# Two interleaved accumulation groups whose upper and lower rows share banks, and a gate of one VectorE product

## The chip, the cores and the metric

The kernel runs on one core of one Trainium2 chip. The metric is the time of one execution on the device in microseconds (us); less is better. The core has TensorE (PE in the profile; PEld is its weight load), VectorE (DVE), ScalarE (ACT), GpSimd (POOL), SyncE (SP), which only issues transfers, and 16 DMA engines. [...]

## What is computed

The reference has two stages over 8 batches of 3200 rows:

```
scores = (1/3200) * z @ z.T            # z: 8 x 3200 x 64
attn   = max(scores, 0) ** 2
x      = u * (attn @ v)                # u, v: 8 x 3200 x 256
wq, wk = x @ w_q, x @ w_k              # 256 -> 64
mixed  = (wq @ wk.T / 8) @ x
out    = max(mixed, 0) @ w_out
```

The kernel never forms `wq @ wk.T`: it sums `wk.T @ x` (64 x 256) over a batch, and multiplies `wq` by that sum later. Nearly all of the work is in the first stage.

## The kernel before, in words

**Tiles.** A batch is cut into 7 groups of output rows (`widths`, L39: six of 512 and one of 128) and 25 tiles of 128 rows (`NT`). For a group `gi` and a tile `ti`, `scores` (L218) multiplies z by itself into PSUM, two tiles at a time (460 such pairs in all), `first_stage` (L238) applies the relu on ScalarE (L242) or VectorE (L246) and leaves `g`, and `second_stage` (L252) squares `g` on ScalarE (L259) or GpSimd (L261) into `at`, an fp16 tile. `at` comes from a ring of `NAT` = 14 buffers (L52). Since the scores are symmetric, a part of the blocks is not computed twice: SyncE issues a transposing DMA from `at` into `tt` tiles (L281), and `weights` (L289) takes a row either from `at` or from `tt`.

**The second product** (`second_product`, L296) multiplies the 128 x 128 blocks of `at` by `v`. Every product is split by rows: the upper 64 partitions (r = 0) and the lower 64 (r = 1) run as two matmuls side by side on the two row halves of the array. [...] A half group (two of the four blocks, `half`) thus has two banks, `acc{half}0` and `acc{half}1`, and one group takes all four accumulation banks (`pacc`). The other four banks hold two `ps` tiles for everything else. A group takes its rows some eight at a time, first for one half, then for the other (`open_rows`, L759); one group is open at a time, and the next begins when the halves' banks are free.

**The gate** (`gate`, L312) runs once per half group: ScalarE copies `acc{half}0` to SBUF (L318), VectorE adds `acc{half}1` (L319), GpSimd multiplies by `u` and writes `x_sb` (L334). For the last two groups VectorE makes a second, dense product (L328). `x_sb` is then transposed by DMA (L348), projected (L365), its keys are transposed (L383) and doubled (L395), and the heads are summed (L402). A batch later come the mixing (L430), the output projection (L457), its eviction by ScalarE (L485) into one of two `fo` buffers, and the store (L486).

**The order** of all instructions is written by a planner in Python, which keeps a clock for each engine: `use_pair` (L584) emits scores, `squares` (L597) chooses ScalarE or GpSimd for each square, `acc_step` (L804) emits two matmuls of the second product, `half_done` (L737) emits the gate and plans the transpose of x, `calm` (L818) holds scores back just before a half group closes, and `move`/`send` (L544, L547) put the transfers into SyncE's queue by due times. The main loop (L866) chooses the next piece of TensorE's work. Every engine then executes its instructions in the order written.

Of the kernel before, what the change touches and what calls it, by code (L numbers as in the profile page):

```python
# [16 lines left out]
def kernel(  # L17
# [34 lines left out]
    NAT = 14  # L52
    NX = 6
    NEARBY = 8
# [10 lines left out]
    psum = ctx.enter_context(tc.tile_pool(name="psum", bufs=3))  # L65
# [11 lines left out]
    def acc_tile(half, r, name, dtype=FP32):  # L77
        n = W if dtype == FP32 else 2 * W
        return pacc.tile([P, n], dtype, tag=f"acc{half}{r}", name=name)

    def top(r):
        return slice(r * dqk, (r + 1) * dqk)
# [204 lines left out]
    accs, xds = {}, {}  # L287
# [8 lines left out]
    def second_product(b, gi, half, ti, first, last):  # L296
        js = range(2 * half, min(2 * half + 2, widths[gi] // P))

        def one(j, r):
            if first and j == js[0]:  # L300
                accs[half, r] = acc_tile(half, r, f"acc{half}{r}")
            nc.tensor.matmul(  # L302
                out=accs[half, r][:, ds((j % 2) * D, D)],
                lhsT=weights(b, gi, ti, j)[top(r), :],
                rhs=vs[b][top(r), ti, :],
                start=(first and j == js[0]),
                stop=(last and j == js[-1]),
            )

        return [lambda j=j: [one(j, r) for r in range(2)] for j in js]  # L310

    def gate(b, gi, half):  # L312
        if (b, gi) not in xs:
            assert len(xs) < NX, (b, gi, list(xs))
            xs[b, gi] = px.tile([P, 2, NC, 2, dh], FP16, tag="x_sb", name="x_sb")
        n = min(2, widths[gi] // P - 2 * half)
        both = psum.tile([P, 2 * D], FP32, tag="both", name="both")
        nc.scalar.copy(out=both[:, 0 : n * D], in_=accs[half, 0][:, 0 : n * D])  # L318
        nc.vector.tensor_add(  # L319
            out=both[:, 0 : n * D], in0=accs[half, 1][:, 0 : n * D], in1=both[:, 0 : n * D]  # L320
        )
        if b == B - 1 and gi >= LASTG - 1:
            if gi < LASTG and half == 0:
                spare = pz.tile([P, NT, 2, dqk], FP16, tag="zd", name="xd")
                spare = spare[:].rearrange("p n a k -> p (n a k)")
                xds[LASTG - 1] = spare[:, 0 : 4 * D].rearrange("p (n d) -> p n d", d=D)
                xds[LASTG] = spare[:, 4 * D : 5 * D].rearrange("p (n d) -> p n d", d=D)
            nc.vector.tensor_mul(  # L328
                out=xds[gi][:, 2 * half : 2 * half + n, :].rearrange("p n d -> p (n d)"),
                in0=both[:, 0 : n * D],  # L330
                in1=us[b, gi][:, 2 * half : 2 * half + n, :].rearrange("p n d -> p (n d)"),
            )
        for r in [half] if widths[gi] == W else range(2):
            nc.gpsimd.tensor_mul(  # L334
                out=xs[b, gi][:, 0:n, :, r, :].rearrange("p n c d -> p (n c) d"),
                in0=both[:, 0 : n * D].rearrange("p (m d) -> p m d", d=dh),
                in1=us[b, gi][:, 2 * half : 2 * half + n, :].rearrange(
                    "p n (c d) -> p (n c) d", d=dh
                ),
            )  # L340
        if 2 * half + n == widths[gi] // P:
            us.pop((b, gi))
# [15 lines left out]
    def halves(gi):  # L358
        return range((widths[gi] // P + 1) // 2)
# [372 lines left out]
    GUARD = 12  # L732
    XDUE = 5.0
    XWAIT = 3.0
    LATE = 0.3

    def half_done(b, gi, half):  # L737
        ready = clock[PE] + FROM_PE
        t = give(ACT, ready, 0.57)
        t = give(DVE, t, 0.68)  # L740
        free_at[half] = t
        t = give(POOL, t, 1.2)
        gate(b, gi, half)
        if half == halves(gi)[-1]:
            n = 8 if widths[gi] == W else 2
            move(
                t + SLACK, t + XDUE, 1.28, 0.21 * n, lambda: turn_x(b, gi),
                lambda t: x_landed(t, b, gi), lambda: len(xTs) < 3,
            )
# [6 lines left out]
    current = {}  # L756
    work, used = [], set()

    def open_rows():  # L759
        if not current.get("left"):  # L760
            if not groups:
                return False
            b, gi = groups.pop(0)
            current.update(b=b, gi=gi, left=list(range(NT)), fresh=True)
            group_begun(b, gi, clock[PE])
        b, gi, left, fresh = (current[x] for x in ("b", "gi", "left", "fresh"))
# [3 lines left out]
        mine = [t for t in ready if (b, gi, t) in made]  # L770
        closing = len(left) <= NEARBY + 1
        want = len(left) if closing else NEARBY
        take = (mine + [t for t in ready if t not in mine])[:want]
        if len(take) < want:
            if closing and len(left) - len(take) < 4:
                take = take[: len(left) - 4]
            if not take or (fresh and len(take) < (6 if b or gi else 2)):
                return False
            if not closing:
                take = take[: max(0, len(left) - 4)]  # L780
        for t in take:
            left.remove(t)
        order = list(halves(gi))
        if fresh and gi == 0 and b > 0:
            order.reverse()
        for half in order:
            for t in take:
                first, end = fresh and t == take[0], not left and t == take[-1]
                todo = second_product(b, gi, half, t, first, end)
                for i, fn in enumerate(todo):  # L790
                    final = i == len(todo) - 1
                    work.append(
                        (
                            fn,
                            (b, gi, half),
                            first and i == 0,
                            end and final,
                            (b, gi, t) if final and half == order[-1] else None,
                        )
                    )  # L800
        current["fresh"] = False
        return True

    def acc_step():  # L804
        if not work and not open_rows():
            return False
        fn, (b, gi, half), begins, closes, row = work[0]
        if begins and free_at.get(half, 0.0) > clock[PE]:
            return False
        work.pop(0)  # L810
        fn()
        clock[PE] += 0.1093 * cold()
        used.add(row)
        if closes:
            half_done(b, gi, half)
        return True

    def calm(weight):  # L818
        steps = next((i for i, x in enumerate(work[:GUARD]) if x[3]), None)
        if steps is None:  # L820
            return True
        shut = clock[PE] + 0.1093 * steps
        first = min(clock[ACT], clock[DVE])
        return max(first, clock[PE] + 0.5) + weight <= shut + LATE

# [7 lines left out]
    make_identity(nc, ident)  # L833
    load_first_z()
# [16 lines left out]
    current.update(b=0, gi=0, left=list(range(NT)), fresh=True)  # L851
    groups.pop(0)
# [7 lines left out]
    group_begun(0, 0, 12.0)  # L860

    total = B * sum(NT * (w // P) for w in widths)
    done_acc = 0
    lead = 140
    turn_about = False
    while groups or work or current["left"]:  # L866
# [18 lines left out]
        wanted = able and p * total < (done_acc + lead) * NPAIR  # L885
        room = room and calm(1.1)
        if room and extra and (not wanted or turn_about or extra[1] == "proj"):
            turn_about = False
            extras.remove(extra)
            extra[2]()  # L890
        elif room and wanted:
            turn_about = True
            use_pair()
        elif acc_step():
            done_acc += 1
# [109 lines left out]
```

## Time and profile before

| | |
|---|---|
| time, median of 3 runs | 803.41 us (803.13 to 806.71) |
| span of the profiled execution | 804.1 us, 0.7 us above that median |
| TensorE busy | 774.2 us, 96% of the span |
| GpSimd busy | 627.2 us, 78% |
| ScalarE busy | 579.3 us, 72% |
| VectorE busy | 467.7 us, 58% |

A busy time is the time in which at least one of an engine's instructions was under way. Since matmuls overlap, TensorE's busy share does not say how near it is to its best pace; the waits, which tell what the engine stood idle for, and the pace of a long run of equal matmuls say more. The chain of work goes back from the last instruction to what released each step. For transfers the profile gives the time of issue on a queue and the landing.

### The profile page before, as it was taken

The numbers are of one execution on the slowest core, as the hardware profiler recorded it, in microseconds if no ns is written. First come the engines' busy times: TensorE is split into PE (matmuls) and PEld (weight loads), VectorE is DVE, ScalarE is ACT, GpSimd is POOL, SyncE is SP. The second block draws the span as 40 slices with busy tenths as digits, with TensorE's granted clock in tenths as the row PEclk, the third lists the DMA queues.
The fourth block names the chain that finished last, engine by engine and source line by source line (L and its number), as shares of the span: only waits on it lengthen the run. The fifth ranks groups of instructions, "written<-read, shape, count | busy, mean of one in ns | idle before, by whom it ended". The sixth has DMA issues, their size and how long they took to land.

```text
span 804.1 us, 28204 instructions
## 1 busy us (share of the span) xinstructions
PE 774.2 (96%) x12373; PEld 657.3 (82%) x12373; DVE 467.7 (58%) x485; ACT 579.3 (72%) x690; POOL 627.2 (78%) x512
## 2 busy tenths in 40 slices
PE   7989999997999999999999999999999999999985
PEld 4879899886888888988888788988889788888863
DVE  4665567553666556755576555765557655564424
ACT  5766888774896777877676768777777676887714
POOL 7887878875788878898878878878877887888730
PEclk9999999999999999999999999999999999999998
DMA  7999999999999988999999989999799998787425
GB/s 188 149 159 174 179 179 156 163 170 192 196 160 206 222 159 166 160 219 196 188 161 186 197 173 200 170 193 201 183 179 162 195 220 165 152 165 171 120 48 216
DMA packets 309356, 141.54 MB, mean 176 GB/s; under 512 B 287728, under 2 KB 290672, under 8 KB 309232
## 3 DMA queue, kind: packets, MB, share of 16 engines
q1 hardware_dynamic: 302320, 123.55, 80.4%
q0 software_dynamic: 6768, 15.98, 14.8%
q8 instruction: 97, 1.59, 0.9%
q14 instruction: 27, 0.22, 0.1%
q10 hardware_dynamic: 144, 0.20, 0.1%
HBM read 59.64 MB, written 26.21 MB: 107 GB/s over the span
## 4 chain that ended last, share of the span: by engine, by line
PE 89%; DVE 4%; DMA 2%; ACT 2%; issue 1%; POOL 1%; POOLq 0%; SPq 0%; DVEq 0%; ACTq 0%
PE acc L302 64%; PE sc L223 12%; PE fo L457 6%; PE qk L365 3%; PE qk L402 2%; DVE g L246 2%; PE mx L430 1%; DMA out_dram<-fo 1%; DMA v_sb<-in_v_dram 1%; DVE hs L424 1%; DVE ha L417 1%; POOL at L261 1%; DVE both L319 1%; ACT both L318 0%; DMA z<-in_z_dram 0%
## 5 line engine op out<-in xcount | busy, mean ns | idle before, releaser
L302 PE MATMUL acc<-v_sb,at 64*128 64x256 f16 x7312 | 495.9, 270 | 4.1 <-DVE both L319 2.5
L261 POOL TENSOR_TENSOR at<-g 128x1024 f16<-128x1024 f32 (+1 forms) x238 | 442.7, 1872 | 72.6 <-DVE g L246 63.3
L302 PEld LDWEIGHTS <-at 64*128 64x128 f16 x7312 | 394.2, 94 | 65.3 <-issue 10.8
L246 DVE TENSOR_SCALAR g<-sc 128x1024 f32<-128x1024 f32 (+1 forms) x285 | 333.9, 1189 | 132.9 <-PE sc L223 118.8
L259 ACT ACTIVATE at<-g 128x1024 f16<-128x1024 f32 (+2 forms) x230 | 233.9, 1026 | 16.6 <-DVE g L246 13.0
L242 ACT ACTIVATE g<-sc 128x1024 f32<-128x1024 f32 x183 | 184.9, 1012 | 60.4 <-PE sc L223 59.3
L334 POOL TENSOR_TENSOR x_sb<-both,u_sb 128x512 f16<-128x512 f32 (+1 forms) x112 | 134.5, 1206 | 72.4 <-DVE both L319 70.4
L223 PE MATMUL sc<-zT 64*128 64x512 f16 x920 | 178.5, 379 | 4.6 <-DVE g L246 3.9
L302 PE MATMUL acc<-v_sb,tt 64*128 64x256 f16 x2304 | 162.2, 269 | 0.0
L319 DVE TENSOR_TENSOR both<-acc,both 128x512 f32<-128x512 f32 (+1 forms) x104 | 69.2, 670 | 136.3 <-ACT both L318 131.4
L302 PEld LDWEIGHTS <-tt 64*128 64x128 f16 x2304 | 123.9, 94 | 11.7 <-issue 0.2
L318 ACT COPY both<-acc 128x512 f32<-128x512 f32 (+1 forms) x104 | 58.1, 564 | 42.8 <-PE acc L302 40.9
L223 PEld LDWEIGHTS <-zT 64*128 64x128 f16 x920 | 57.7, 94 | 18.6 <-issue 14.8
L485 ACT ACTIVATE fo<-fo 128x1024 f32<-128x1024 f32 (+2 forms) x50 | 45.4, 909 | 34.1 <-PE fo L457 27.6
L447 ACT ACTIVATE rt<-mx 128x1024 f16<-128x1024 f32 (+1 forms) x49 | 45.7, 934 | 23.1 <-PE mx L430 23.0
L378 ACT CAST qk<-qk 128x512 f16<-128x512 f32 (+1 forms) x54 | 29.4, 545 | 36.7 <-PE qk L402 28.1
L457 PE MATMUL fo<-wo,rt 128*128 128x256 f16 x400 | 53.4, 274 | 1.2 <-ACT rt L445 0.6
L457 PEld LDWEIGHTS <-rt 128*128 128x128 f16 x400 | 34.7, 98 | 15.8 <-issue 9.8
L417 DVE TENSOR_TENSOR ha<-qk,ha 128x512 f32<-128x512 f32 x38 | 26.2, 690 | 33.2 <-ACT qk L378 33.0
L365 PE MATMUL qk<-xT_sb,wqk 64*128 64x256 f16 (+1 forms) x404 | 32.1, 265 | 0.0
L402 PE MATMUL qk<-x_sb,kx 64*128 64x256 f16 x368 | 29.6, 269 | 0.0
L395 POOL COPY kx<-kx 128x128 f16<-128x128 f16 (+1 forms) x101 | 26.1, 288 | 3.0 <-DMA kx<-qk 3.0
(44 smaller groups left out, 225.4 us busy)
## 6 DMA issues: line engine op xcount, KB each, us to landing
u_sb<-in_u_dram SPq DMA_DIRECT2D x48, 512.0 KB, 4.8
out_dram<-fo SPq DMA_DIRECT2D x45, 512.0 KB, 4.8
v_sb<-in_v_dram POOLq DMA_DIRECT2D x35, 320.0 KB, 6.1
zn<-in_z_dram POOLq DMA_DIRECT2D x7, 400.0 KB, 5.9
tt<-at SPq DMA_TRANSPOSE x144, 4.2
out_dram<-fo SPq DMA_DIRECT2D x6, 256.0 KB, 2.1
u_sb<-in_u_dram SPq DMA_DIRECT2D x8, 128.0 KB, 3.3
out_dram<-fo SPq DMA_DIRECT2D x8, 128.0 KB, 2.5
```

The source lines that it names most:

```text
L223: nc.tensor.matmul(out=sc[:, h, 0:gw], lhsT=zT[b][top(h), ts(ti, P)], rhs=zT[b][top(h), ds(gs, gw)], start=True, stop=True,)
L242: nc.scalar.activation(out=g[:, hs, 0:w], in_=sc[:, hs, 0:w], func=RELU, scale=GSCALE)
L246: nc.vector.tensor_scalar(out=g[:, hs, 0:w], in0=sc[:, hs, 0:w], scalar1=0.0, scalar2=GSCALE, op0=AOP.max, op1=AOP.mult,)
L259: nc.scalar.square(out=out, in_=g[:, hs, 0:w])
L261: nc.gpsimd.tensor_mul(out=out, in0=g[:, hs, 0:w], in1=g[:, hs, 0:w])
L302: nc.tensor.matmul(out=accs[half, r][:, ds((j % 2) * D, D)], lhsT=weights(b, gi, ti, j)[top(r), :], rhs=vs[b][top(r), ti, :], start=(first ...
L318: nc.scalar.copy(out=both[:, 0 : n * D], in_=accs[half, 0][:, 0 : n * D])
L319: nc.vector.tensor_add(out=both[:, 0 : n * D], in0=accs[half, 1][:, 0 : n * D], in1=both[:, 0 : n * D])
L334: nc.gpsimd.tensor_mul(out=xs[b, gi][:, 0:n, :, r, :].rearrange("p n c d -> p (n c) d"), in0=both[:, 0 : n * D].rearrange("p (m d) -> p m ...
L365: nc.tensor.matmul(out=ps[:, r, 0 : n * P], lhsT=wqk[top(r), c, :, :].rearrange("p t h -> p (t h)"), rhs=xTs[b, gi][top(r), 0:n, c, :], st ...
L447: nc.scalar.activation(out=out, in_=ps[:, 0:nr, 0 : ND * n * P], func=RELU)
L457: nc.tensor.matmul(out=banks[r][:, ds(j * D, D)], lhsT=flat[:, ds((dc * n + j) * P, P)], rhs=wo[:, dc, :], start=(dc == 0 and j == 0), sto ...
```

## The change

1. **Banks.** A group keeps two banks instead of four, one per half group. In phase 0 the upper rows add into half 0 and the lower rows into half 1; in phase 1 it is the other way round (`k = r ^ phase`). Each of the 25 tiles is used once in each phase.
2. **Two groups open.** The other two banks hold a second group (`turn = i % 2`). A list of stages says which group and phase comes next: a group's first 12 tiles in phase 0, then the 13 tiles in phase 0 that the group before it has left, then 25 tiles in phase 1, and so on. The very first group has 25 tiles in phase 1 and then 25 in phase 0. The group of width 128 has one phase and still uses two banks and the sum.
3. **Changes through ScalarE.** At the end of a stage ScalarE copies one element (`sign_off`), which waits for the last product; the first product after the change waits for that copy. There are 95 such copies.
4. **The gate.** VectorE multiplies a bank by `u` and writes `x_sb` directly, two instructions per group, 94 in all. The last group of width 512 writes a dense x and GpSimd copies it. Only the groups of width 128 keep the copy, the sum and GpSimd's product.
5. **Sizes.** The ring of `at` tiles has 16 buffers instead of 14, the pool for the sums 2 instead of 3. `NEARBY`, `GUARD`, `LATE` and `calm` are gone.

```diff
-    NAT = 14
+    NAT = 16
...
-    psum = ctx.enter_context(tc.tile_pool(name="psum", bufs=3))
+    psum = ctx.enter_context(tc.tile_pool(name="psum", bufs=2))
...
+    def sign_off(g):
+        seen = nc.scalar.copy(out=sign[:, 1:2], in_=sign[:, 0:1])
+        tc.add_manual_dep(seen.ins, g["wrote"].ins.name, SEES, reason="last before the change")
+        g["seen"] = seen
+
+    def second_product(g, ti, phase, j):
+        b, gi = g["b"], g["gi"]
+        whole = widths[gi] == W
+        change = whole and g["last"] not in (None, phase)
+        for r in range(2):
+            k = r ^ phase
+            if not g["given"][k]:
+                g["acc"][k] = acc_tile(k, g["turn"], f"acc{k}{g['turn']}")
+            g["given"][k] += 1
+            product = nc.tensor.matmul(
+                out=g["acc"][k][:, ds(j * D, D)],
+                lhsT=weights(b, gi, ti, 2 * k + j if whole else 0)[top(r), :],
+                rhs=vs[b][top(r), ti, :],
...
+            if change and r == 0:
+                tc.add_manual_dep(
+                    product.ins, g["seen"].ins.name, SEES, reason="the change of halves"
+                )
+        g["last"], g["wrote"], g["seen"] = phase, product, None
...
-        nc.scalar.copy(out=both[:, 0 : n * D], in_=accs[half, 0][:, 0 : n * D])
-        nc.vector.tensor_add(
-            out=both[:, 0 : n * D], in0=accs[half, 1][:, 0 : n * D], in1=both[:, 0 : n * D]
-        )
...
+                    nc.vector.tensor_mul(
+                        out=out,
+                        in0=g["acc"][k][:].rearrange("p (m d) -> p m d", d=dh),
+                        in1=u2.rearrange("p n (c d) -> p (n c) d", d=dh),
+                    )
...
+    def stages_of(i):
+        if widths[groups[i][1]] != W:
+            return [[i, 0, 12], None, [i, 0, 13]]
+        if i == 0:
+            return [None, [i, 1, 25], [i, 0, 25]]
+        return [[i, 0, 12], [i, 1, 25], [i, 0, 13]]
...
+    stages = [parts[0][1]]
+    for i in range(len(groups)):
+        nxt = parts[i + 1] if i + 1 < len(groups) else [None] * 3
+        stages += [nxt[0], parts[i][2], nxt[1]]
...
+            if len(g["left"]) == 2 and g["last"] not in (None, phase):
+                if g["seen"] is None or g["seen_at"] > clock[PE]:
+                    continue
```

The planner writes a new order for everything, so scores, squares, gates, projections and transfers all stand at other places than before. The numbers of matmuls and of transfers are the same.

More of the change, by code (lines that the diff above doesn't have):

```diff
@@ L294, in weights @@
         return turned[b, gj, gi][:, j, ti - starts[gj] // P, :]
[L296 to L304, printed above, removed]
+    sign = consts.tile([1, 2], FP32, tag="sign", name="sign")
@@ L781, in open_rows @@
[L781 to L800, printed above, removed]
@@ L801, in open_rows @@
-        current["fresh"] = False
-        return True
[L804 to L824, printed above, removed]
+        return ready
@@ new lines, in choose @@
+    def choose():
+        seen = set()
+        for stage in stages[:AHEAD]:
+            i, phase, _ = stage
+            b, gi = groups[i]
+            if i in seen:
+                continue
+            seen.add(i)
+            g = opened.get(i)
+            if g is None:
+                if not may_open(i) or len(ready_rows(b, gi, range(NT))) < (FRESH if i else 2):
+                    continue
+                begun[0] += 1
+                g = open_group(i)
+            if len(g["left"]) == 2 and g["last"] not in (None, phase):
+                if g["seen"] is None or g["seen_at"] > clock[PE]:
+                    continue
+            ready = ready_rows(b, gi, g["left"][phase])
+            if not ready or (i > min(opened) and sum(map(len, g["left"])) == 1):
+                continue
+            other = g["left"][1 - phase] if len(g["left"]) == 2 else []
+            first = len(other) == NT
+            t = min(ready, key=lambda t: (t in other, ((b, gi, t) in made) == first))
+            g["left"][phase].remove(t)
+            stage[2] -= 1
+            if not stage[2]:
+                stages.remove(stage)
+            n = 2 if widths[gi] == W else 1
+            over = n == 2 and other and (stage not in stages or not g["left"][phase])
+            work.extend((g, t, phase, j, j == n - 1, t not in other, over) for j in range(n))
+            return True
+        return False
```

184 lines of the change are left out of this document (108 added, 76 removed).

## Prediction

> **What bounds the kernel now.** I read the busy times first, then the chain of work, the pace of TensorE in a long run of products, and then TensorE's waits.
>
> ```profile
> PE 774.2 (96%) x12373; PEld 657.3 (82%) x12373; DVE 467.7 (58%) x485; ACT 579.3 (72%) x690; POOL 627.2 (78%) x512
> ...
> PE 89%; DVE 4%; DMA 2%; ACT 2%; issue 1%; POOL 1%; POOLq 0%; SPq 0%; DVEq 0%; ACTq 0%
> ```
> ```profile
> 756.12 1.91 PE L302 MATMUL acc<-v_sb,tt 64*128 64x256 f16 x32
> ```
> ```profile
> PE mx L430 <- ACT fo L485: 4.5, 1, 4.5
> PE ztp L125 <- ACT zd L119: 4.0, 1, 4.0
> PE sc L223 <- DVE g L246: 3.9, 6, 1.0
> PE hd L402 <- POOL kx L395: 2.9, 1, 2.9
> PE acc L302 <- DVE both L319: 2.5, 6, 0.5
> PE ztp L125 <- POOL zd L119: 1.1, 1, 1.1
> PE acc L302 <- DMA v_sb<-in_v_dram: 0.8, 1, 0.8
> ...
> PE acc L302 <- ACT both L318: 0.5, 1, 0.5
> ...
> PE sc L223 <- ACT g L242: 0.2, 1, 0.2
> ```
>
> TensorE is 89% of the chain. The 32 products are 16 pairs, side by side; 1.91 us less the 0.27 us of the last one is 1.64 us for 15.5 pairs, so a pair takes some 0.109 us (0.106 to 0.11 by how the ends are counted). The change leaves the number of products as it was. So it can only gain what TensorE waits for, or lose by new waits. All waits together are 21 us; those at the start (4.0, 1.1, 0.8) come before any product and stay. What the change can reach is the rest: gates 2.5 + 0.5 = 3.0 us, scores 3.9 + 0.2 = 4.1, the wait for `fo` 4.5, the heads at the end 2.9.
>
> **The engines beside TensorE.** Rows by shape:
>
> ```profile
> L259 ACT ACTIVATE at<-g 128x1024 f16<-128x1024 f32 x218 | 229.0, 1057 | 16.6 <-DVE g L246 13.0
> L242 ACT ACTIVATE g<-sc 128x1024 f32<-128x1024 f32 x179 | 183.4, 1024 | 59.8 <-PE sc L223 58.6
> L318 ACT COPY both<-acc 128x512 f32<-128x512 f32 x96 | 55.2, 580 | 39.1 <-PE acc L302 37.5 <-PE sc L223 1.4
> ...
> L378 ACT CAST qk<-qk 128x128 f16<-128x128 f32 x7 | 1.9, 272 | 0.1
> ```
> ```profile
> L246 DVE TENSOR_SCALAR g<-sc 128x1024 f32<-128x1024 f32 x273 | 328.6, 1220 | 132.5 <-PE sc L223 118.8 <-POOL at L261 7.9 <-POOL x_sb L334 4.0
> L319 DVE TENSOR_TENSOR both<-acc,both 128x512 f32<-128x512 f32 x96 | 65.8, 691 | 128.5 <-ACT both L318 123.7 <-PE sc L223 4.7
> ...
> L328 DVE TENSOR_TENSOR xd<-both,u_sb 128x512 f16<-128x512 f32 x2 | 1.4, 692 | 0.1
> ```
> ```profile
> L261 POOL TENSOR_TENSOR at<-g 128x1024 f16<-128x1024 f32 x234 | 439.9, 1892 | 72.6 <-DVE g L246 63.3 <-issue 3.7 <-ACT g L242 2.3
> L334 POOL TENSOR_TENSOR x_sb<-both,u_sb 128x512 f16<-128x512 f32 x96 | 122.9, 1283 | 63.8 <-DVE both L319 61.8 <-DMA tt<-at 1.2
> ```
>
> In the order as built, ScalarE loses 96 copies (96 x 0.580 = 55.7 us), 27 large squares (28.5) and 14 relus (14.3), and gets 95 copies of one element. No row shows so small an operation; it lies between nothing and the 0.272 us of the 128-column row, so 26 us at most: ScalarE ends some 73 us or more lighter. GpSimd loses 96 products (123 us) and gets 27 large squares (51 us): 70 us lighter. VectorE changes 96 sums of 0.691 us for 96 products; the row of L328 has their shape but reads SBUF, L319 reads a bank: both say 0.69, so nothing, and 14 relus more are 17 us. None of this is on the chain: at 58 to 78% these engines cost TensorE only where something comes late. I count all of it as nothing, since TensorE's 89% hides it; if that cover went, GpSimd would be next with 557 us, far below.
>
> **What goes.**
> (a) Gates. A bank was wanted again 18 pairs, about 2 us, after its half closed, and ScalarE, VectorE had to finish in that. Now a group's banks are wanted after the next group's 25 tiles of phase 1, 50 pairs or 5.5 us. The path is two products of 0.69 us. -3.0 us, within 0 and -3.0; the distance is so large that I take all.
> (b) Waits of scores for VectorE's relu. They came from sums that stood in VectorE's queue. The two products per group stand there too, back to back (1.38 us). Between 0 and -4.1, I take half: -2.0.
> (c) The wait for `fo`:
>
> ```profile
> 165.78 1.03 ACT L485 ACTIVATE fo<-fo 128x1024 f32<-128x1024 f32 x1
> ```
> ```profile
> 180.34 1.08 SPq L486 DMA_DIRECT2D out_dram<-fo  x2
> ```
> ```profile
> 180.34 8.14 DMA out_dram<-fo
> ...
> 188.56 0.39 ACT fo L485
> 188.95 0.04 issue
> 188.99 0.61 PE mx L430 x4
> ```
> ```profile
> ACT fo L485 <- DMA out_dram<-fo: 6.4, 1, 6.4
> ```
> ```profile
> 184.00:189.00 5.00, 0.49 (x10) 0.19 (x5) 1.23 (x1) 0.44 (x2) 2.12 (x2) 0.97 1.20 267
> 189.00:194.00 5.00, 5.00 (x52) 3.65 (x53) 0.36 (x1) 2.35 (x4) 0.52 (x2) 0.69 1.13 190
> ```
>
> ScalarE had written this `fo` at 166.8; its store left SyncE's queue at 180.3, behind transposes whose inputs were not there yet, and landed at 188.5. There are two `fo` buffers, so the third eviction, and then TensorE, waited. In the window after it the granted clock is 0.69 (column after the five engines): 5.0 x 0.31 = 1.6 us more. The price is 4.5 + 1.6 = 6.1 us. In the new order this store is entry 104 of SyncE's list instead of 102, some 4 us later at 2 us an entry (400 entries in 804 us), but its `fo` is made about 10 us of TensorE's work later, so the lag shrinks by 6 us to about 15; the buffer is wanted again 13.4 us of work later (18.3 before), less 1.6 as the narrow group's projection is short, and TensorE felt the wait 1.9 us after ScalarE (6.4 against 4.5). 15 - 11.8 - 1.9 = 1.3 us are left. Bounds: -6.1, or +4.9 if the lag stays and only the distance shrinks. I take 1.3 - 6.1 = -4.8.
>
> **What comes.**
> (d) The start. Before, each tile of the first group fed four pairs as soon as it was there; now two, since the first stage is all 25 tiles in phase 1, and nothing else may open before.
>
> ```profile
> 11.00:24.00 13.00, 12.15 (x163) 9.50 (x164) 1.00 0.66 137
> ```
> ```profile
> 9.22 3.76 POOL L261 TENSOR_TENSOR at<-g 128x1024 f16<-128x1024 f32 x2
> 13.87 1.89 POOL L261 TENSOR_TENSOR at<-g 128x1024 f16<-128x1024 f32 x1 [0.89 <-DVE g L246]
> ```
>
> The first row is L302 alone: 81 pairs from 11 to 24 us. In the new order GpSimd makes 7 of the first 13 squares, the last of them for the last tile of that stage. Its third cannot start much before 13.8, as its scores are issued no earlier, and five at 1.892 end at 23.3; two pairs and the first change follow, so at 24.0 TensorE has done 50 pairs: 31 fewer, 3.4 us. Lower bound 1.5 us (third square right behind the second, and a share of later waits absorbed), upper 5. I take +3.3.
> (e) 95 changes. ScalarE's copy waits for the product, behind it wait squares and relus, and for them GpSimd and SyncE; TensorE's queue stands behind the next product.
>
> ```profile
> ACT both L318 <- PE acc L302: 40.9, 42, 7.2
> ```
>
> L318 waited in the same way, and in 42 of 104 cases ScalarE was already there. Then the latency is 0.16 (a product's 0.27 beyond the pace) + 0.05 + 0.27 + 0.05 (hand-over, from 188.95 to 188.99 above) = 0.53 us. With half a square ahead it is 1.06, with a whole one 1.59. In the order, other work stands between: in the middle case 3.5 us; ten of the 95 have less than 1.6 (0, 0.43 twice, 0.87 twice, 1.09, 1.31 three times, 1.52). The stalls are then 0.7 us in sum, 2.7, or 6.8. By the 42 of 104: 0.4 x 0.7 + 0.6 x 2.7 = 1.9. I take +1.9.
>
> ```profile
> L302 PEld LDWEIGHTS <-at 64*128 64x128 f16 x7312 | 394.2, 94 | 65.3 <-issue 10.8
> ```
>
> [...]
> (f) The end.
>
> ```profile
> 773.86 2.17 PE L302 MATMUL acc<-v_sb,ttl 64*128 64x256 f16 x35
> 778.97 0.86 PE L402 MATMUL hd<-x_sb,kx 64*128 64x256 f16 x8 [2.93 <-POOL kx L395]
> ```
>
> The heads wait for the last keys, through ScalarE, a transpose and GpSimd. Before, 3.1 us of work covered part of that path, now 1.95 us, as the last groups close closer together: +1.2, or +0.5 if GpSimd's last products set it as before. The longer stall may slow the clock behind it by up to the 1.6 us above. I take +1.5, within 0 and +2.8.
> (g) Transposed rows are used about 19 us of work after their scores, before 33. A row takes 1.2 (relu) + 1.9 (square) + its wait in SyncE's queue + a landing:
>
> ```profile
> tt<-at SPq DMA_TRANSPOSE x144, 4.2
> ```
> ```profile
> SPq L281 <- ACT g L242: 56.9, 20, 16.7
> ```
>
> 7.3 us and a mean wait of 2.8, at worst 16.7: few come late. +0.5, within 0 and +4.
>
> **The sum.** -3.0 - 2.0 - 4.8 + 3.3 + 1.9 + 1.5 + 0.5 = -2.6 us, from 804.1 to 801.5 us of span. The median of the runs is 0.7 below that span: **800.8 us**, 0.3% less. A measurement of this kernel tells about 0.5%, 4 us, from no change.
>
> **Rivals.**
> 1. *All waits go and little comes back.* (b) at -4.1, (c) at -6.1, (d) at +1.5, (e) at +0.7, the rest nothing: 804.1 - 11.0 - 0.7 = 792.4 us. For it: all other engines get lighter. Against: the first stage of the new order, and covers under 0.53 us.
> 2. *The store still holds TensorE up.* (c) is 0: 806.3 - 0.7 = 805.6 us. For it: SyncE's queue is in order and its lag in this stretch was 13.5 us. Against: the later place of the `fo`.
> 3. *ScalarE answers late, and the changes become the wait* (slower). If a relu and a square stand ahead of the copy, the latency is 0.53 + 1.02 + 1.06 = 2.6 us, and the stalls of the order's short covers sum to 19 us: 800.8 - 1.9 + 19 = 818 us; with one square, 805.7. It decides from about 2 us on. For it: 62 of 104 copies found ScalarE not yet free. Against: ScalarE gets 73 us lighter.
>
> **How the numbers follow.** The forecast has a chance of 0.45, from 797 to 804, a third of it below 799.4; rival 1 0.25; rival 2 0.13, most within 0.5%; rival 3 0.17, with 807.4 passed. So faster 0.39, same 0.42, slower 0.19. The range reaches down to rival 1, and up to the forecast with (e) at a whole square and (f) and (g) at their upper bounds, 800.8 + 4.9 + 1.3 + 3.5 = 810.5, and a little into rival 3: 792 to 812.
>
> **What would show it.** (a) no product waits for VectorE's gate. (b) scores' waits near 2 us. (c) no wait of `fo` for a store at batch 1 and no clock below 0.9 there. (d) L302 has about 100 matmuls, not 163, from 11 to 24 us, with waits for GpSimd's squares. (e) products wait for ScalarE's copy for some 2 us, at the groups next to the narrow one. (f) the heads wait about 4 us. It would be wrong if products waited for rows in the middle of the run, if a pair took longer than 0.109 us in the new bank order, or if SyncE's queue fell behind elsewhere.

## The result, and the profile after

The changed kernel takes 798.25 us (median of 20 executions, 793.31 to 801.82) against 802.25 us for the kernel before (20 executions, 797.53 to 808.41). The ratio is 0.9944, 95% interval 0.992 to 0.9968: 0.3 to 0.8% less. The forecast was 800.8 us, the range 792 to 812.

The profiled execution has a span of 796.5 us; the one of before had 804.1. This pair misleads: the two profiles differ by 7.6 us, the medians by 4.0. In the changed kernel's 20 executions the time is 1.8 to 1.9 us above the span, so a span of 804.1 us belongs to an execution of about 806 us, well above the median of the kernel before.

Busy times and the chain of the changed kernel, from its page:

```profile
PE 771.0 (97%) x12373; PEld 657.6 (83%) x12373; DVE 477.8 (60%) x493; ACT 502.0 (63%) x642; POOL 565.0 (71%) x456
...
PE 85%; POOL 4%; DMA 4%; DVE 3%; ACT 2%; issue 1%; SPq 0%; DVEq 0%; POOLq 0%; ACTq 0%
```

ScalarE is 77 us lighter and GpSimd 62, VectorE 10 heavier; TensorE is still the chain. TensorE's waits in the changed kernel (us in total, times, longest):

```profile
PE ztp L124 <- DVE zd L118: 5.1, 1, 5.1
PE sc L222 <- DVE g L245: 3.1, 7, 1.0
PE hd L428 <- POOL kx L421: 2.9, 1, 2.9
PE qk L391 <- DMA xT_sb<-x_sb: 1.2, 1, 1.2
PE acc L314 <- DMA tt<-at: 1.0, 1, 1.0
...
PE acc L314 <- POOL at L260: 0.6, 2, 0.5
...
PE acc L314 <- ACT sign L301: 0.4, 1, 0.4
PE acc L314 <- DVE x_sb L350: 0.3, 1, 0.3
```

The wait of `mx` for `fo` (4.5) is gone, and of the gates' 3.0 us one wait of 0.3 is left. One single product waited for the copy at a change. New are two transposes that landed late. TensorE's first work came 1.0 us later than before (the first row, 5.1 us instead of 4.0). Windows on L314 alone (busy, matmuls, then loads, the granted clock, DMA share, GB/s):

```profile
11.00:24.00 13.00, 8.29 (x100) 5.48 (x99) 1.00 0.71 141
24.00:60.00 36.00, 33.60 (x540) 26.10 (x540) 1.00 1.11 163
```

At the start 100 matmuls stand where before had 163; from 24 to 60 us there are 540, where before had 471. Set against before at equal work of TensorE (each matmul counted at its undisturbed pace), the changed kernel is 0.6 us late after 5 us of work, 3.6 late after 15, 2.4 late after 25, 2.0 ahead after 90, 8.0 ahead after 210, and 7.6 ahead at the end. Some 2 us are thus gained by 90 us of work, some 6 at the wait for the store, and nothing after that: of the seven waits for gates in the kernel before, five lie in its first 88 us.

### The profile page after: what moved, and what is told of

It is laid out like the page before. It is cut to its first block, busy times and chain, and to the rows that moved or that the text cites. A ratio compares the mean times of both kernels' runs of the same rounds, so it can differ in the third digit from the quotient of the medians.

```text
span 796.5 us, 28102 instructions
## 1 busy us (share of the span) xinstructions
PE 771.0 (97%) x12373; PEld 657.6 (83%) x12373; DVE 477.8 (60%) x493; ACT 502.0 (63%) x642; POOL 565.0 (71%) x456
## 4 chain that ended last, share of the span: by engine, by line
PE 85%; POOL 4%; DMA 4%; DVE 3%; ACT 2%; issue 1%; SPq 0%; DVEq 0%; POOLq 0%; ACTq 0%
PE acc L314 61%; PE sc L222 11%; PE fo L483 6%; POOL at L260 3%; PE qk L391 3%; PE qk L428 2%; DVE g L245 2%; PE mx L456 2%; DMA xT_sb<-x_sb 1%; DMA tt<-at 1%; DMA v_sb<-in_v_dram 1%; ACT g L241 1%; DMA z<-in_z_dram 0%; DVE hs L450 0%; ACT at L258 0%
## 5 line engine op out<-in xcount | busy, mean ns | idle before, releaser
L260 POOL TENSOR_TENSOR at<-g 128x1024 f16<-128x1024 f32 (+1 forms) x275 | 499.6, 1832 | 176.4 <-DVE g L245 122.5
L314 PE MATMUL acc<-v_sb,at 64*128 64x256 f16 x7312 | 490.6, 269 | 1.6 <-POOL at L260 0.6
L245 DVE TENSOR_SCALAR g<-sc 128x1024 f32<-128x1024 f32 (+1 forms) x295 | 348.8, 1201 | 190.4 <-PE sc L222 171.7
L314 PEld LDWEIGHTS <-at 64*128 64x128 f16 x7312 | 389.8, 94 | 57.3 <-issue 6.0
L241 ACT ACTIVATE g<-sc 128x1024 f32<-128x1024 f32 (+1 forms) x173 | 171.0, 993 | 102.2 <-PE sc L222 96.7
L258 ACT ACTIVATE at<-g 128x1024 f16<-128x1024 f32 x193 | 200.5, 1049 | 25.8 <-DVE g L245 23.4
L222 PE MATMUL sc<-zT 64*128 64x512 f16 x920 | 181.9, 379 | 3.8 <-DVE g L245 3.1
L314 PE MATMUL acc<-v_sb,tt 64*128 64x256 f16 x2304 | 163.9, 269 | 1.0 <-DMA tt<-at 1.0
L314 PEld LDWEIGHTS <-tt 64*128 64x128 f16 x2304 | 124.8, 94 | 16.8 <-DMA tt<-at 1.3
L350 DVE TENSOR_TENSOR x_sb<-acc,u_sb 128x512 f16<-128x512 f32 x94 | 60.2, 682 | 21.8 <-PE acc L314 17.9
L301 ACT COPY sign<-sign 1x1 f32<-1x1 f32 x95 | 17.2, 182 | 38.5 <-PE acc L314 38.5
L314 PE MATMUL acc<-v_sb,ttl 64*128 64x256 f16 x384 | 26.9, 269 | 0.0
```

The costliest lines, as they stand in the source:

```text
L222: nc.tensor.matmul(out=sc[:, h, 0:gw], lhsT=zT[b][top(h), ts(ti, P)], rhs=zT[b][top(h), ds(gs, gw)], start=True, stop=True,)
L241: nc.scalar.activation(out=g[:, hs, 0:w], in_=sc[:, hs, 0:w], func=RELU, scale=GSCALE)
L245: nc.vector.tensor_scalar(out=g[:, hs, 0:w], in0=sc[:, hs, 0:w], scalar1=0.0, scalar2=GSCALE, op0=AOP.max, op1=AOP.mult,)
L258: nc.scalar.square(out=out, in_=g[:, hs, 0:w])
L260: nc.gpsimd.tensor_mul(out=out, in0=g[:, hs, 0:w], in1=g[:, hs, 0:w])
L314: product = nc.tensor.matmul(out=g["acc"][k][:, ds(j * D, D)], lhsT=weights(b, gi, ti, 2 * k + j if whole else 0)[top(r), :], rhs=vs[b][to ...
```

## Experiments

"The kernel before" and "the changed kernel" are the two above; each ratio is to runs of the kernel before made for that comparison, whose medians were 800.98 to 801.81 us.

### 1. The kernel before, with a third `fo` buffer

```diff
-            fo = pg.tile([P, 2, W], FP32, tag="fo", name="fo", bufs=2)
+            fo = pg.tile([P, 2, W], FP32, tag="fo", name="fo", bufs=3)
```

> The kernel before with three fo buffers instead of two, its order untouched (to make room two weights are loaded into x_sb buffers and the pool for the sums has two buffers). Theory (step c): the wait of the mixing of batch 1 for the store, 4.5 us and 1.6 us of low clock behind it, stands in every execution and goes: the median falls by 5 to 6 us, ratio about 0.993. Rival: the profiled execution was one of the slow ones of the kernel before (806 us against a median of 802.3), the stall is not in most executions, and the median falls by under 2 us, ratio 0.998 or more.

799.67 us (12 executions, 797.66 to 804.84) against 801.43; ratio 0.9968, interval 0.9939 to 0.9996. The span of its profile is 797.1 us, and the windows in which before stood still are full, at full clock:

```profile
184.00:189.00 5.00, 4.88 (x76) 3.68 (x72) 2.45 (x2) 2.47 (x4) 2.36 (x2) 1.00 1.14 272
189.00:194.00 5.00, 5.00 (x92) 4.69 (x88) 1.26 (x2) 2.70 (x4) 2.52 (x4) 1.00 1.21 221
```

At this place the trace gains 5.9 us on that of before, as worked out (6.1). But the median falls by 1.8. The executions suggest why: of these 29 of the kernel before 11 are above 804 us, with the third buffer 1 of 12; over all five sets of runs of the kernel before 29 of 114 are. So the stall costs some 6 us in the profiled execution, and seems to be in a quarter to two fifths of the executions. That is inferred from the times: only one execution of before was traced, and experiment 12, with its third buffer, has executions 5 us and more above its fastest ones too. In the one trace the price is as the theory had it; in the median the fall lies at the rival's bound of 2.

The interval, 0.9939 to 0.9996, overlaps that of the changed kernel, 0.992 to 0.9968. So the kernel before with a third buffer is not told apart from the changed kernel. In the traces the difference is 2.1 us: at 700 us of work this one is 5.6 us ahead of before, the changed kernel 7.7.

### 2. The changed kernel with 14 `at` buffers

```diff
-    NAT = 16
+    NAT = 14
```

> The changed kernel with the ring of at tiles at 14 again. Theory: the gain is waits of gates and of the store that are gone, the ring has no part in it: within 2 us of the changed kernel, some 4 us under the kernel before. Rival: the two open groups hold their rows longer, and only the longer ring makes up for it: scores wait, TensorE runs out of rows, 5 us or more are lost, and the time is that of the kernel before or above it.

803.68 us (797.85 to 807.56), ratio 1.001 (0.9982 to 1.0039): the whole gain is gone, as the rival said. The order is dealt anew, so not all of it is the ring. In the profile the kernel is 0.7 us behind before after 45 us of work, where three executions in the changed kernel's order (its own, experiments 10 and 11) are 1.0 to 1.7 ahead: products wait 1.2 us for GpSimd's square and 1.5 for `sign` in the first 37 us. Another 3.8 us is a wait of the heads for keys. GpSimd's rows about it:

```profile
111.59 0.59 POOL L143 DMA_DIRECT2D zn<-in_z_dram  x1
112.68 3.74 POOL L260 TENSOR_TENSOR at<-g 128x1024 f16<-128x1024 f32 x2 [0.50 <-DVE g L245]
121.76 0.53 POOL L421 COPY kx<-kx 128x128 f16<-128x128 f16 x2 [5.33 <-DMA kx<-qk]
```

GpSimd idles 5.33 us, because the transpose of the keys landed 9.6 us after its issue (3.6 in the median of the changed kernel), with a load of 400 KB of z issued at 111.6. The same wait stands at the same place, 2.0 us long, in experiment 11, which has 16 buffers. So some 2 us is what the trace shows of the ring; the rest is not separated. The other half of the question was not run: what 16 buffers would give the kernel before. Without it, a part of the gain may belong to the ring and not to the banks and the two open groups.

### 3 and 5. Five copies at a change: answered late, or only busy

In the first, the change waits for the fifth copy; in the second for the first, and the other four follow.

```diff
-        seen = nc.scalar.copy(out=sign[:, 1:2], in_=sign[:, 0:1])
+        for i in range(5):
+            seen = nc.scalar.copy(out=sign[:, 1:2], in_=sign[:, 0:1])
```
```diff
         g["seen"] = seen
+        for i in range(4):
+            nc.scalar.copy(out=sign[:, 1:2], in_=sign[:, 0:1])
```

> The changed kernel with five one-element copies in a row at each change instead of one, at the same place of the order: the first product after the change waits for the fifth. At 0.182 us a copy that is 0.73 us more of latency per change and 95 x 0.73 = 69 us more of ScalarE, nearly its load of before. Theory: changes are hidden by 3.5 us of other products in the middle case; by the short covers of the order (0, 0.43 twice, 0.87 twice, 1.09, 1.31 three times) the stalls grow by about 3 us; no loss comes from ScalarE's load. Rival (a late ScalarE and full engines set the time): 10 us or more, as relus and squares come late too.

> The changed kernel with five one-element copies at each change, but the first product after the change waits for the first of them alone; the other four only keep ScalarE busy, 69 us in all, right behind it. With the five copies in a chain the kernel took 808.7 us, 10.4 more than the changed kernel. Theory L (latency: what counts is how late the change is answered): most of the 10 us is gone, within 3 us of the changed kernel. Rival O (occupancy: what counts is that squares and relus stand behind longer copies): 6 to 10 us stay, as ScalarE has the same work.

The chain of five: 808.69 us, ratio 1.0075 (1.0047 to 1.0104). The four behind: 804.65 us, ratio 1.0042 (1.002 to 1.0064). So of 10.4 us 6.4 stay when nothing waits for the extra copies, or 7.9 of 10.5 by the ratios: O was right about the larger part. The rest, 2.6 to 4 us, is latency; in the first trace products wait 4.8 us for `sign` instead of 0.4. TensorE's waits of the second:

```profile
PE sc L222 <- ACT g L241: 3.1, 8, 0.7
...
PE mx L458 <- ACT rt L475: 1.0, 3, 0.4
...
PE acc L316 <- ACT sign L301: 0.4, 1, 0.4
```

The change itself waits no more than in the changed kernel; scores and mixings wait for relus, 4.1 us where there were 0.2, since relus stand right behind the extra copies. ScalarE's total is 568.5 us, below the 579.3 of before, so the total alone does not explain the loss. The planner counts 0.1 us for a change and did not know of the extra copies. That this is the reason was not tested: no run gave the planner their cost.

### 4. One group open at a time

```diff
-        return i == begun[0] and len(opened) < 2 and all(
+        return i == begun[0] and len(opened) < 1 and all(
...
-    stages = [parts[0][1]]
-    for i in range(len(groups)):
-        nxt = parts[i + 1] if i + 1 < len(groups) else [None] * 3
-        stages += [nxt[0], parts[i][2], nxt[1]]
-    stages = [x for x in stages if x]
+    stages = [x for p in parts for x in p if x]
```

> The changed kernel with only one group open at a time: a group does 12 tiles of phase 0, 25 of phase 1, 13 of phase 0, then the next begins in the other two banks. Each of the 95 changes has only scores and projections to stand behind. Theory: the interleaving is what hides the changes; one that has nothing to stand behind costs 0.4 to 0.6 us, so up to 38 to 57 us, about half of it where scores stand between: 15 to 35 us slower than the changed kernel. Rival: scores cover the changes anyway and the second open group is not needed: within 4 us of the changed kernel.

857.67 us (4 executions), ratio 1.0687 (1.063 to 1.0745): 59 us above the changed kernel, more than the 15 to 35 expected. Its waits, and the rows of matmuls and of loads of L314 with what they stood idle for:

```profile
PE acc L314 <- ACT sign L301: 12.9, 31, 0.9
PE sc L222 <- DVE g L245: 8.8, 20, 1.1
PE qk L391 <- DMA xT_sb<-x_sb: 6.3, 6, 2.5
```
```profile
L314 PE MATMUL acc<-v_sb,at 64*128 64x256 f16 x7312 | 488.1, 270 | 16.5 <-ACT sign L301 12.9 <-POOL at L260 1.6 <-DMA v_sb<-in_v_dram 0.7
L314 PEld LDWEIGHTS <-at 64*128 64x128 f16 x7312 | 370.3, 94 | 91.1 <-ACT sign L301 33.1 <-issue 4.3 <-POOL at L260 2.6
```

The sharing of banks thus lives on the second open group. The changes alone hold products for 12.9 us and the loads for 33.1. The waits of scores and projections are longer too; that no other products fill in when scores or x come late is the likely reason, not shown by itself.

### 6 and 9. The gate back on ScalarE and GpSimd, then with a third `fo` buffer

```diff
-                    nc.vector.tensor_mul(
-                        out=out,
-                        in0=g["acc"][k][:].rearrange("p (m d) -> p m d", d=dh),
+                    both = psum.tile([P, 2 * D], FP32, tag="both", name="both")
+                    nc.scalar.copy(out=both[:], in_=g["acc"][k][:])
+                    nc.gpsimd.tensor_mul(
+                        out=out,
+                        in0=both[:].rearrange("p (m d) -> p m d", d=dh),
```

> The changed kernel with shared banks and two open groups, but the gate back on ScalarE (copy of a bank to SBUF) and GpSimd (product with u), with the planner's costs to match; ScalarE has 55 us more, GpSimd some 120 us more or squares pushed to ScalarE, and x comes about 1 us later. Theory: a bank is wanted again 5.5 us after its group closes, so no gate wait returns and engines off the chain cost nothing: within 2 us of the changed kernel. Rival O (the lighter engines are the gain, as the chain of five copies hints): 4 to 10 us slower, with waits of scores for relus on ScalarE and of changes for sign.

> The kernel with the gate back on ScalarE and GpSimd (807.3 us), its order untouched, with three fo buffers instead of two (room from smaller pools that nothing waits for). In its profile the waits of the mixing for the store were 2.2 and 1.0 us and the clock fell behind them; up to 330 us it stood as well as the changed kernel. Theory S (the gate itself is free, the late store is what it costs): 4 to 6 us fall, to 801 to 803 us, and no wait for a store is left. Rival O (the load of ScalarE and GpSimd costs by late relus and squares): under 2 us fall, 805.5 us or more.

807.33 us, ratio 1.0065 (1.0035 to 1.0095), and with the third buffer 804.76, ratio 1.0049 (1.0032 to 1.0066). No product waits for a gate in either, so the two pairs of banks, not the single VectorE product, took the gates' waits away. Up to 330 us both traces are level with the changed kernel or a little ahead. What came then, in the kernel with two buffers:

```profile
PE mx L458 <- DVE g L245: 3.6, 1, 3.6
PE mx L458 <- ACT fo L513: 3.2, 2, 2.2
...
PE sc L222 <- ACT g L241: 0.8, 3, 0.4
```

The 9 us fit O's size. Its waits for relus on ScalarE are only 0.8 us, and `sign` holds products for 0.4 as in the changed kernel, so that reason fails. The wait for the store is S's, and the third buffer removes it; the median fell by 2.6 (1.3 by the ratios), less than the 4 to 6 of S, to a time between the two forecasts. What stays is the 3.6, in both. Around it in experiment 9 stand VectorE's rows, then GpSimd's, then the window behind it, with the granted clock after the five engines:

```profile
619.22 5.06 DVE L452 TENSOR_TENSOR hs<-ha 128x256 f16<-128x256 f32 x1
624.20 1.21 DVE L245 TENSOR_SCALAR g<-sc 128x1024 f32<-128x1024 f32 x1
```
```profile
618.39 5.59 POOL L260 TENSOR_TENSOR at<-g 128x1024 f16<-128x1024 f32 x3
```
```profile
625.50:630.00 4.50, 4.50 (x50) 3.79 (x51) 1.23 (x1) 2.36 (x4) 1.89 (x1) 0.62 1.00 189
```

The sum `hs`, which takes 0.42 us alone, took 5.06, until three squares of GpSimd in a row had ended (618.39 + 5.59 = 623.98; `hs` ended at 624.28). The relu behind it came late, TensorE stood 3.6 us, and the granted clock was 0.62 for the 4.5 us after (1.7 us). In the traces this one place is the whole difference: after 575 us of work experiment 9 is 7.0 us ahead of before and the changed kernel 7.5, after 600 they are 2.9 and 8.6 ahead. In the medians it is not: 804.76 less 3.6 and 1.7 is 799.5, and by the ratios some 3 us stay open. The late relu is on VectorE, behind GpSimd's squares, so the rival of experiment 9 (late relus and squares) has a part in it. Whether GpSimd's heavier load or only the new order put three squares in a row there is open, and `hs` elsewhere was not run with this gate.

### 7 and 8. Another first group

```diff
     stages = [x for x in stages if x]
+    stages[:3] = [[0, 1, 4], [0, 0, 8], [0, 1, 8], [0, 0, 17], [1, 0, 12], [0, 1, 13]]
```
```diff
+    stages[:3] = [[0, 1, 9], [0, 0, 25], [1, 0, 12], [0, 1, 16]]
```

> The changed kernel with another first group: 4 tiles in phase 1, 8 in phase 0, 8 in phase 1, 17 in phase 0, then group 1 begins and the last 13 tiles follow; scores also wait in the planner for z of the next batch. A tile then feeds both phases early, as before the change. Theory (step d): the lag of 2.4 us at 25 us of TensorE's work against the kernel before falls to about 0 to 1, at the price of changes with nothing to stand behind (0.4 to 0.5 us each); behind it the order is dealt again, so the end may move by 3 us either way; if nothing else happens 796 us. Rival: the ring of 16 is the limit at the start, not the phases; the lag stays above 2 us.

> The same with one early change only: 9 tiles in phase 1, 25 in phase 0, then group 1 begins, then the last 16 tiles in phase 1. Theory (step d): 18 pairs of the second phase become available from 9 tiles, so the lag at 25 us of work falls to 0 to 1.5 us; if nothing else happens some 796 to 797 us. Rival: as in the kernel with four early changes, the lag stays above 2 us.

Both kernels also hold scores back in the planner until z of the next batch is there.

797.54 us, ratio 0.9954 (0.9925 to 0.9982), and 797.14, ratio 0.994 (0.9896 to 0.9983): not told apart from the changed kernel. L314 from 11 to 24 us, in this order:

```profile
11.00:24.00 13.00, 9.23 (x110) 6.66 (x111) 1.00 0.74 150
```
```profile
11.00:24.00 13.00, 9.92 (x128) 7.49 (x127) 0.87 0.71 141
```

The lag after 25 us of work is 1.7 and 1.9 us instead of 2.4. The first products started at 11.2 and 11.7 us, in the changed kernel at 11.3. In the second the granted clock, with all engines in view, was low at the start:

```profile
11.00:16.00 5.00, 4.30 (x40) 2.89 (x40) 2.50 (x3) 2.82 (x3) 3.35 (x2) 0.66 1.09 218
```

That is worth 5.0 x 0.34 = 1.7 us, nearly all of its lag. Experiment 12, with the same first group and the same low clock there, has a lag of 1.3. So the phases are a part of the start's loss: 0.7 us by experiment 7, up to 2.2 by experiment 8 if its clock is taken out. How much is not settled, and the whole is too small for the median.

### 10. The changed kernel with a third `fo` buffer

The edit is that of experiment 1.

> The changed kernel with three fo buffers, its order untouched. Theory S: in the changed kernel's order the store comes in time in nearly every execution, so nothing is left to gain: within 1 us of the changed kernel, ratio to the kernel before 0.993 to 0.996. Rival: its slower executions (up to 801.8 us) still wait for the store: the median falls by 1.5 to 3 us, to 796 us.

796.45 us (795.66 to 800.18), ratio 0.9934 (0.9902 to 0.9967). The median is 1.8 us lower, the ratio overlaps that of the changed kernel: not settled. Set against experiment 1, the same two kernels without any wait for the store, it is 0.9934 / 0.9968 = 0.9966, some 2.7 us, with some 3.5 us to either side by the two intervals: not clear of nothing.

### 11. The sum `hs` on GpSimd

```diff
-        nc.vector.tensor_add(out=hss[b][:], in0=ha[:, 0, :], in1=ha[:, 1, :])
+        nc.gpsimd.tensor_add(out=hss[b][:], in0=ha[:, 0, :], in1=ha[:, 1, :])
```

> The changed kernel with the last sum of the heads, hs, on GpSimd instead of VectorE, at the same place of the order. In the profile this sum of 128x256 with two SBUF inputs takes 0.42 us alone and up to 1.62 us, until 0.3 us after the square that GpSimd has under way, and the relu and the scores behind it are late: scores waited 0.57 us behind it at 146.8 us and 1.02 us at 710, a mixing 0.25. Theory P (VectorE's sum and GpSimd's squares hold each other up): these waits go, 1 to 2 us less. Rival: hs then stands behind squares in GpSimd's queue, the mixing waits for it, and the time rises by 1 us or more.

796.11 us (792.21 to 802.8), ratio 0.9943 (0.9915 to 0.997). The same group in the changed kernel, then here:

```profile
L450 DVE TENSOR_TENSOR hs<-ha 128x256 f16<-128x256 f32 x7 | 8.1, 1155 | 0.2
```
```profile
L450 POOL TENSOR_TENSOR hs<-ha 128x256 f16<-128x256 f32 x7 | 5.1, 725 | 5.7 <-DVE ha L443 5.7
```

The scores' waits for relus on VectorE fall from 3.1 to 1.0 us, those at 146.8 and 710 us are gone, and no mixing waits: P is right about the waits. The profiled execution, one of the longer ones (800.38), lost 3.5 us to late transposes (1.5 for x, 2.0 for keys). Five of its 12 executions are below 794.1 us, of the changed kernel's 20 two. By the ratio the two are not told apart.

### 12. All three together

Experiments 8, 10 and 11 in one kernel.

> The changed kernel with three things together: the first group as 9 tiles of phase 1, 25 of phase 0, 16 of phase 1; three fo buffers; the sum hs on GpSimd. Theory (each takes a different wait: the start 0.5, the store up to 1.8 in the median, hs 1.6 us): they add up, 3 to 4 us less than the changed kernel, ratio to the kernel before 0.988 to 0.991. Rival (what differs from execution to execution are late landings of transposed tiles, which none of the three touches): the three add up to 1 us at most, ratio 0.993 to 0.995.

794.34 us (792.67 to 807.29), ratio 0.9934 (0.9897 to 0.997). Seven of 12 executions take 792.7 to 794.3 us, five 798.1 to 807.3. By the median it is 3.9 us under the changed kernel, as theory said, by the ratio the rival fits: it beats the kernel before, but not the changed one beyond doubt. The profiled execution (798.06) shows what the slower ones carry:

```profile
PE qk L391 <- DMA xT_sb<-x_sb: 5.0, 4, 2.5
```

The changed kernel has 1.2 us there. Such waits differ between executions of one order: experiment 10, with the changed kernel's order, waited 1.9 us for `tt` and 0.2 for `xT_sb`, where that waited 1.0 and 1.2.

## Why the prediction was right, and where not

The sign was right, and the waits that were to go are gone from the trace; the time was 2.5 us too high. That 800.8 came so near is in part luck. In the median the store is worth 2 to 3 us less than the 4.8 taken, and what comes, (d) to (g), was taken at 7.2 us and measured 4.6 in the trace, so the two errors cancel. By its steps:

(a) **Gates**, -3.0: 2.7 gone. Right, and by the reason given, the distance of the banks: with the old engines (experiments 6 and 9) they stay gone.

(b) **Scores**, -2.0: 4.1 became 3.3, of which some 1.2 belong to the start; about -2 besides. The size is right, the cause is not. The prediction blamed the sums of the gate in VectorE's queue. None of the six waits in the kernel before stands behind such a sum. Three (1.03, 1.03 and 0.45 us) stand behind `hs`, one behind another sum of the heads, and at two VectorE had been idle before the relu. VectorE's and GpSimd's rows at one of the longest:

```profile
431.72 1.63 DVE L424 TENSOR_TENSOR hs<-ha 128x256 f16<-128x256 f32 x1
433.27 1.21 DVE L246 TENSOR_SCALAR g<-sc 128x1024 f32<-128x1024 f32 x1
```
```profile
431.18 1.88 POOL L261 TENSOR_TENSOR at<-g 128x1024 f16<-128x1024 f32 x1 [0.67 <-DVE g L246]
```

The square ends at 433.06, `hs` at 433.35. The changed kernel has the same at 708.49, with 1.62 us. Experiment 11 shows the link: with `hs` on GpSimd the waits behind it are gone.

(c) **The store**, -4.8: in the two profiles all of it goes, some 6 us, and from 184 to 194 us the clock is 1.00. The forecast of what would be left (1.3) was a little too careful. In the median it is worth about 2 (experiment 1), most likely since the wait is not in every execution. This is the largest error behind the right result: the profile of before was taken for the typical execution. The prediction set the median 0.7 us below the span; but times lie 1.8 to 1.9 us above spans, so the profiled execution took about 806 us, some 2.5 above the median of the three runs, which themselves ranged from 803.1 to 806.7. That was a sign of a slow execution.

(d) **The start**, +3.3: 50 pairs from 11 to 24 us, as worked out, and 3.6 us of lag after 15 us of work; +2.4 remains after 25. Right, with two additions: 0.6 us of the lag stood already after 5 us of work, and one gate wait of the kernel before, at 28.17 us, falls within these 25 us. How much of it the phases are stays open (experiments 7 and 8).

(e) **95 changes**, +1.9: 0.4. This term was mis-sized. One change had nothing to stand behind and waited 0.37 us; the others, from 0.43 us of cover on, show no wait of a product. ScalarE's rows:

```profile
L301 ACT COPY sign<-sign 1x1 f32<-1x1 f32 x95 | 17.2, 182 | 38.5 <-PE acc L314 38.5
```

The copy takes 0.182 us, not up to 0.272. At the change that waited, a square stood just ahead of the copy on ScalarE, but the copy still began 0.15 us after the last product had ended (24.16 and 24.01 us). Nor did every change hold up a weight load: one load takes 0.094 us in the row of L314's loads, so 95 of them would be 8.9 us, and the trace has 1.1 us of idle time of these loads put down to `sign`, in three waits. Rival 3 was a real mechanism that this order avoids: 0.73 us more of latency cost 2.6 to 4 us, where 3 were expected, and the copies' occupancy 6.4 to 7.9 (experiments 3 and 5).

(f) **The end**, +1.5: 2.9 us in both. The keys' last copy stands in GpSimd's queue behind the narrow group's two products, which need the kernel's last product of all. In the changed kernel:

```profile
769.32 1.64 POOL L363 TENSOR_TENSOR x_sb<-both,u_sb 128x256 f16<-128x256 f32 x2 [1.24 <-DVE both L358]
770.90 0.52 POOL L421 COPY kx<-kx 128x128 f16<-128x128 f16 x2
```

Before, the same pair stood at 777.03. So the work that covers the keys' path does not matter; the prediction had named this case and priced it at +0.5, and it is 0.

(g) **Transposed rows**, +0.5: 1.0 for `tt` and 1.2 for `xT_sb`, within the bounds, too small as taken. These waits change from one execution to the next (experiments 10 to 12).

Costing the lighter engines at nothing is shown in part: with the gate back on the old engines the traces are level up to 330 us, but in the median these two kernels are 6 to 9 us slower than the changed kernel, and the traces explain the larger part by the places named there. It failed for the extra copies of experiment 5. That the ring was given no term was an omission: some 2 us at the start hang on it, and with 14 buffers nothing is left of the gain (experiment 2).

So where did the gain go? Of about 4.5 us by the ratio some 2 to 2.6 are the store, by experiment 1 (0.3 to 4.9 by its interval); some 2 to 2.7 are gates and scores less the start and the late transposes, by the traces and by experiments 1 and 10. In the times this second part is not clear of nothing; that the gates' waits are gone is seen in the traces alone. The steps as measured in the two profiles sum to -2.7 - 2 - 6 + 2.4 + 0 + 2.2, with 0.4 of (e) within the start: -6.1 of the 7.6. Part of what is missing is that the table of waits counts less than a wait costs. In the kernel before:

```profile
40.68 0.27 PE L302 MATMUL acc<-v_sb,at 64*128 64x256 f16 x1
41.41 0.83 PE L302 MATMUL acc<-v_sb,at 64*128 64x256 f16 x12 [0.46 <-DVE both L319]
```

From start to start are 0.73 us where the pace is 0.109, so 0.62 are lost and 0.46 are listed: 0.16 us more at this wait.

## What to carry to other kernels

Before a stall is priced from one profile, look at the spread of the runs: the wait for the store, some 6 us in the one trace of the kernel before, was worth 1.8 us in the median, most likely since it is in a part of the executions only. Set the profiled execution's own time, not its span, against the median. Two accumulators shared banks at almost no cost, 0.4 us of waits in the trace, where a second open group supplied the products between a change and its answer; with one open group the kernel was 59 us slower. All these kernels let only one row half at a time add into a bank; what happens without such turns was not shown. Work on an engine that is off the chain was not free where relus stood right behind it: 380 copies that the order's planner had not counted cost 6.4 us, with that engine's total below what it was before.

## What the runs showed of the hardware

- VectorE's sum `hs`, which has two SBUF inputs, took 0.42 us where no square of GpSimd was under way (at 241.40 and 526.81 us of the kernel before), 1.62 and 1.63 beside one square, and 5.06 beside three in a row (experiments 6 and 9). Beside one square and beside the three it ended 0.3 us after the last. Between squares back to back the traces show two cases. At 619 us of experiment 9 the sum ended only after two further squares that began later than it by their rows. In the changed kernel it got in between two:

```profile
329.43 1.13 DVE L450 TENSOR_TENSOR hs<-ha 128x256 f16<-128x256 f32 x1
```
```profile
328.38 3.93 POOL L260 TENSOR_TENSOR at<-g 128x1024 f16<-128x1024 f32 x2 [0.73 <-POOL at L260]
```

  There the pair of squares took 3.93 us instead of the 3.74 of the pair in experiment 2. What decides is open.
- The granted clock, 0.69 in the 5 us behind the wait of 4.5 us in the kernel before, was low behind some shorter waits too. In experiment 11 the granted clock was 0.66 in the 5 us from 120.5 us, after a wait of 2.0 us, in experiment 6 it was 0.66 from 376 to 381 us, after 2.2 us. In experiment 12 it was 1.00 behind a wait of 2.5 us at 324 us. Behind the same wait both were seen: the heads' wait at the end is 2.9 us in the kernel before and in experiment 1, and the granted clock behind it is 0.66 and 1.00 in these two windows:

```profile
779.00:784.00 5.00, 4.75 (x28) 1.92 (x28) 1.54 (x3) 1.77 (x2) 0.14 (x1) 0.66 0.14 28
```
```profile
773.40:778.40 5.00, 4.05 (x33) 2.17 (x34) 1.62 (x4) 2.20 (x3) 0.13 (x1) 1.00 0.12 26
```

  What decides is open.
- A copy of one element on ScalarE took 0.182 us in the changed kernel, five in a row 0.188 each on average (experiment 3).
